# A fused attention-plus-MLP kernel on one core: the first block in two column parts, another load order, a zero tile for warming, and new planner ranks

## Chip, core and metric

The kernel runs on one core of one Trainium2 chip. The metric is the device time of one execution in microseconds; of several executions the median counts. The profile is of one such execution, with its instructions, DMAs and waits.

## What is computed

The input x has 2048 rows (positions) of 640 numbers in bf16. It is normalized row by row, and two branches use the result: an attention over eight earlier positions with a stride of two, and an MLP of width 1536. Their sum with x is the output.

```python
def reference(A_x, A_wqkv, A_wo, B_x, B_w1, B_b1, B_w2, B_b2):
    x = A_x
    xn = _layernorm(x, axis=-1)
    return x + _A_ref(xn, A_wqkv, A_wo) + _B_ref(xn, B_w1, B_b1, B_w2, B_b2)

# A: 32 heads of 20; W, dil = 8, 2
qkv = (x @ wqkv) split into q, k, v per head
logits = einsum("bhsd,bhswd->bhsw", q, kg) * scale     # kg: k at s, s-2, ..., s-14
attn = softmax(where(mask, logits, -1e9))
o = einsum("bhsw,bhswd->bhsd", attn, vg);  A = o @ wo
# B
h = gelu(x @ w1 + b1);  B = h @ w2 + b2
```

B_x is not used: both branches work on the normalized A_x.

## The kernel before

The rows go through in four chunks of 512 (n = 0 to 3), each of four blocks of 128 (bl). Most intermediates are kept transposed, with features on the partitions: xnT is the normalized x of a chunk as five column tiles (KT = 5) of 128 features by 512 positions.

Of each chunk these pieces are done. The planner's names for them are given, because the prediction goes by them.

- st, rs, rc, xn: statistics on VectorE, square root on ScalarE, reciprocal on VectorE, and the normalized block. In chunk 0 this is done block by block, and xn on VectorE; in the other chunks the square root is taken for four blocks at once, and xn is on ScalarE.
- tp and tc: in chunk 0 TensorE transposes a block in five steps (L424), and ScalarE copies the result to xnT. In the other chunks tc is a transposing DMA on the queue of SP.
- gj and gc: the q, k and v projections of chunk 0, by block, in five groups of column tiles (GROUPS): g = 0 is q tiles 0 to 3, g = 1 k tiles 0 to 3, g = 2 the last tiles of q and k, g = 3 and 4 are v. ScalarE copies the sums from PSUM. In the other chunks pj and pc do this for a whole chunk, one column tile at a time (five matmuls of 128x512, L463).
- qk and lg: VectorE multiplies q with a shifted k (L513, eight per chunk), and TensorE sums over each head's features (L539).
- m, mx, ex, ss, ri, at: the softmax on VectorE, with the exponential on ScalarE.
- xs and xd: the weights (attn) are copied out to all features of their head, the tile ax, by two DMAs issued by ScalarE and two issued by SP. There is one ax buffer.
- av, ad, ot: VectorE multiplies ax with a shifted v (L612, eight per chunk), adds in three steps (L621) and makes oT (L627). There is one oT buffer.
- f1 and ge: the first MLP matmul (L634, 12 tiles per chunk) and GELU on ScalarE (L645).
- o: for each block the second MLP matmul in four pieces of three hidden tiles, and a fifth piece that adds oT times wo (L665, L667). oc copies the result from PSUM, od adds it to the output in memory.
- xb: VectorE adds b2 to x (L440), and SP writes the chunk to the output (L447). ld is three loads (w2, wo and b2) that SP issues once the four transposes of chunk 1 have been issued (L335 to L337).

The work around the change is ordered by a planner, `Plan.run`, which runs while the kernel is built. Each piece has an engine, an assumed duration, a rank, needs, and buffers. The planner goes forward in its own time and gives each free engine the piece of the lowest rank that can start. The kernel issues its instructions in that order, and each engine then works through its list strictly in order, on real semaphores. RANK holds offsets that are added to the ranks of some pieces; by its entries the whole list is shifted. `land` are the planner's assumptions of when loads have landed. They set the order only; on the chip an instruction waits for the load itself.

The pool psA has four PSUM accumulators ("acc") that transposes, projections and f1 take in turn. So a projection can wait until ScalarE has copied the one that is four back.

Before the first piece, TensorE runs WARM matmuls on the identity tile (L706), whose results aren't used. The identity is made by GpSimd (POOL) in two steps.

Loads are issued at the start, in this order on the queue of SP: x block 0, wq, x blocks 2 and 3, wk, wv, b1, x of chunks 1 to 3, w1 (L321 to L331). x block 1 is issued by ScalarE (L322).

Of the kernel before, what the change touches and what calls it, by code (L numbers as in the profile page):

```python
# [133 lines left out]
LASTB = S // P - 1  # L134
WARM = 40

# [4 lines left out]
RANK = {  # L141
# [3 lines left out]
}  # L145


def make_plan(fns, offsets=RANK):

    pl = Plan(offsets)  # L150
# [6 lines left out]
    def f(kind, *a):  # L157
        return lambda: fns[kind](*a)
# [6 lines left out]
    for n in range(NCH):  # L165
# [6 lines left out]
        for bl in range(BPC):  # L172
            land = (3.2, 3.2, 6.6, 6.6)[bl] if n == 0 else 11.4 + 1.9 * n
            pl.add(f"st{n}{bl}", VE, 1.17, -40 if n else -99, [], f("st", n, bl), after=land)
            if n == 0:
                pl.add(f"rs{n}{bl}", SE, 0.35, -99, [f"st{n}{bl}"], f("sqrt", n, bl, bl + 1), table="sqrt")
                pl.add(f"rc{n}{bl}", VE, 0.17, -99, [f"rs{n}{bl}"], f("rstd", n, bl, bl + 1))
# [3 lines left out]
        for bl in range(BPC):  # L181
            xn, tp = ("xn", n, bl), ("acc", "tp", n, bl)
            pl.add(f"xn{n}{bl}", SE if n else VE, 0.81 if n else 0.42, early + -4.0 if n else -99, [f"rc{n}" if n else f"rc{n}{bl}"], f("xn", n, bl), [xn])
            if n > 0:
                pl.add(f"tc{n}{bl}", DQ, 4.0 if n > 1 else 2.7, early - 3.0, [f"xn{n}{bl}"], f("td", n, bl), [xn, xnT], 21.5)
                continue
            pl.add(f"tp{n}{bl}", PE, 0.3, early + -3.0 if n else -99, [f"xn{n}{bl}"], f("tp", n, bl), [xn, tp])
            pl.add(f"tc{n}{bl}", SE, 0.65, early + -3.0 if n else -99, [f"tp{n}{bl}"], f("tc", n, bl), [tp, xnT])
        if n == 1:
# [3 lines left out]
        if n == 0:  # L193
            for bl in range(BPC):
                for g, parts in enumerate(GROUPS):
                    ps, last = ("acc", "g", bl, g), max(p[0] for p in parts)
                    tos = sum(p[2] - p[1] for p in parts)
                    land = (5.9, 9.2, 11.5)[last]
                    r = -50 + (last == 2)
                    pl.add(f"gj{bl}{g}", PE, 0.28 * tos, r, [f"tc0{bl}"], f("gj", bl, g), [xnT, ps], land)  # L200
                    pl.add(f"gc{bl}{g}", SE, (0.27, 0.54, 0, 0.54)[tos - 1], -50, [f"gj{bl}{g}"], f("gc", bl, g), [ps] + [(q, k, v)[p[0]] for p in parts])
# [70 lines left out]
def kernel(  # L272
# [65 lines left out]


    ident = consts.tile([P, P], BF16, name="ident")  # L340
    make_identity(nc, ident[:])
# [38 lines left out]
    def do_st(n, bl):  # L380
        b = n * BPC + bl
        stats = lnp.tile([P, 2, nc.vector.BN_STATS_DIM], F32, tag="stats", name="stats")
        nc.vector.bn_stats(stats[:, 0, :], x_sb[:, b, 0 : D // 2])  # L383
        nc.vector.bn_stats(stats[:, 1, :], x_sb[:, b, D // 2 : D])
        nc.vector.bn_aggr(mv[:, b, :], stats[:])

# [13 lines left out]

    def do_xn(n, bl):
        b = n * BPC + bl
        xn = lnp.tile([P, D], BF16, tag="xn", name="xn")
        tiles["xn", n, bl] = xn
        if n:
            nc.scalar.activation(
                xn[:], x_sb[:, b, :], ACT.Identity, bias=nmr[:, b : b + 1], scale=rstd[:, b : b + 1]
            )
            return
        nc.vector.tensor_scalar(  # L410
            out=xn[:],
            in0=x_sb[:, b, :],
            scalar1=mv[:, b, 0:1],
            scalar2=rstd[:, b : b + 1],
            op0=ALU.subtract,
            op1=ALU.mult,
        )

    def do_tp(n, bl):
        xn = tiles["xn", n, bl]  # L420
        tp = psA.tile([P, 2 * CH], BF16, tag="acc", name="tp")
        tiles["tp", n, bl] = tp
        for t in range(KT):
            nc.tensor.transpose(tp[:, t * P : (t + 1) * P], xn[:, t * P : (t + 1) * P], ident[:])  # L424

    def do_tc(n, bl):
        xnT = get(("xnT", n), lambda: xtp.tile([P, KT, CH], BF16, tag="xnT", name="xnT"))
        nc.scalar.copy(
            xnT[:, :, bl * P : (bl + 1) * P],
            tiles["tp", n, bl][:, 0 : KT * P].rearrange("p (t m) -> p t m", t=KT),  # L430
        )
# [38 lines left out]

    def do_gj(bl, g):
        if bl == 0 and g == 3:
            bias1()
        cs = slice(bl * P, (bl + 1) * P)
        ps = psA.tile([P, BPC, P], F32, tag="acc", name="gps")
        tiles["gps", bl, g] = ps
        slots = [(which, to) for which, a, b in GROUPS[g] for to in range(a, b)]
        for i, (which, to) in enumerate(slots):
            for ti in range(KT):
                nc.tensor.matmul(  # L480
                    ps[:, i, :],
                    lhsT=wqkv_p[which][:, ti, to, :],
                    rhs=tiles["xnT", 0][:, ti, cs],
                    start=(ti == 0),
                    stop=(ti == KT - 1),
                )

# [251 lines left out]
```

## Time and profile before

| what | us |
|---|---|
| median of 6 runs (216.47 to 217.9) | 217.06 |
| the profiled execution | 218.04 |
| its span, first to last instruction | 215.9 |
| TensorE busy (PE) | 207.2 |
| VectorE busy (DVE) | 180.7 |
| ScalarE busy (ACT) | 107.4 |
| first projection matmul of chunk 0 starts | 7.63 |
| first f1 matmul starts | 25.18 |
| first product with ax starts | 60.95 |
| first oT starts | 82.27 |
| last matmuls end | 212.82 |

How to read it: times of single steps come from the profiled execution and are in microseconds from the start of the span. A line of a timeline holds start, duration, engine, line of the kernel, operation, tile written and tiles read, shapes, count, and in brackets how long the engine idled before and what ended it. A matmul's drawn end lies behind the moment at which the next one starts, since they are pipelined; so the pace of a row of matmuls is read from their starts. The chain that ended last is followed back from the last instruction; a line has start, duration, and what held the chain. PEclk is the granted clock of TensorE in tenths of full speed.

### The profile page before, as it was taken

The page shows a single profiled execution, that of the slowest core. Times are in us where ns is not written, and L with a number is a line of the kernel's source. Part 1 is how long each engine was busy: PE and PEld are TensorE (multiplying, and loading weights), DVE is VectorE, ACT ScalarE, POOL GpSimd, SP SyncE. Part 2 cuts the span into 40 slices and gives each one's busy share as a digit, 9 for nine tenths or more (in the row PEclk, how much of TensorE's full clock was granted, in tenths as well). Part 3 has the DMA queues.
Part 4 walks back from the last instruction along what each step waited for, and adds up shares of the span by engine and source line. Part 5 has one row for each costly group of instructions (what it writes and reads, how often), then busy time and mean ns, then how long its engine had stood idle before and what let it go on. Part 6 is the DMA issues. An engine that isn't in the chain of part 4 may idle for free.

```text
span 215.9 us, 3941 instructions
## 1 busy us (share of the span) xinstructions
PE 207.2 (96%) x1669; PEld 121.0 (56%) x1692; DVE 180.7 (84%) x170; ACT 107.4 (50%) x190; POOL 14.5 (7%) x33
## 2 busy tenths in 40 slices
PE   7799999999999999999999989999999999999994
PEld 7799845554454444655655545566445455555552
DVE  3829999679989999999999999998999999982001
ACT  3676994895928375553176075213763521351210
POOL 2000000000000000100011000111100011101220
PEclk9999999999999999999999999999999999999999
DMA  6999408826972112508120370222112522205223
GB/s 216 365 365 357 87 20 254 322 98 126 250 62 56 35 30 33 152 0 187 44 30 3 39 183 3 30 33 30 16 18 20 174 30 27 29 8 121 33 30 62
DMA packets 21449, 21.49 MB, mean 100 GB/s; under 512 B 9016, under 2 KB 18616, under 8 KB 21432
## 3 DMA queue, kind: packets, MB, share of 16 engines
q1 hardware_dynamic: 17832, 16.49, 27.7%
q0 software_dynamic: 2160, 2.46, 9.7%
q10 hardware_dynamic: 1440, 2.29, 3.7%
q8 instruction: 13, 0.21, 0.4%
q14 instruction: 4, 0.03, 0.1%
HBM read 10.00 MB, written 5.08 MB: 70 GB/s over the span
## 4 chain that ended last, share of the span: by engine, by line
PE 51%; DVE 29%; DMA 13%; SPq 2%; issue 2%; ACTq 1%; ACT 1%; DVEq 0%
PE lo L665 18%; PE hps L634 14%; DVE pv L612 10%; PE gps L480 8%; DMA ax<-attn 6%; PE hi L667 6%; DMA b2bc<-in_B_b_dram 5%; DVE pv L621 4%; DVE prod L513 3%; PE pps L463 3%; DVE ssum L574 3%; DVE x_sb L440 2%; DVE attn L586 2%; DMA x_sb<-in_A_x_dram 1%; DVE rs L581 1%
## 5 line engine op out<-in xcount | busy, mean ns | idle before, releaser
L634 PE MATMUL hps<-xnT,w_sb 128*128 128x512 bf16 x236 | 54.2, 379 | 0.2
L665 PE MATMUL lo<-w_sb,hT 128*128 128x512 bf16 x183 | 51.9, 379 | 0.0
L612 DVE TENSOR_TENSOR pv<-vT,ax 128x2560 bf16<-128x2560 bf16 x32 | 45.8, 1485 | 1.3 <-DMA ax<-attn 1.3
L513 DVE TENSOR_TENSOR prod<-qT,kT 128x2560 bf16<-128x2560 bf16 x32 | 45.5, 1483 | 0.1
L667 PE MATMUL hi<-w_sb,hT 128*128 128x128 bf16 x192 | 40.3, 219 | 0.5
L645 ACT ACTIVATE hT<-hps,b1T 128x512 bf16<-128x512 f32 x48 | 31.6, 686 | 15.6 <-PE hps L634 13.6
L634 PEld LDWEIGHTS <-w_sb 128*128 128x128 bf16 x240 | 22.9, 98 | 26.5
L621 DVE TENSOR_TENSOR pv<-pv 128x5120 bf16<-128x5120 bf16 x12 | 33.8, 2822 | 0.3
L665 PEld LDWEIGHTS <-hT 128*128 128x128 bf16 x192 | 18.7, 98 | 22.7 <-issue 0.6
L672 ACT CAST osb<-lo 128x512 bf16<-128x512 f32 x15 | 8.8, 585 | 42.7 <-issue 22.8
L678 POOL DMA_DIRECT2D out_dram<-osb x15 | 13.1, 873 | 195.1 <-ACT osb L673 195.1
L665 PE MATMUL lo<-wo,oT 128*128 128x512 bf16 x77 | 22.6, 379 | 0.0
L667 PEld LDWEIGHTS <-hT 128*128 128x128 bf16 x192 | 18.4, 98 | 1.5
L463 PE MATMUL pps<-xnT,wv_sb 128*128 128x512 bf16 x72 | 17.4, 379 | 1.2 <-ACT vT L498 1.0
L463 PE MATMUL pps<-xnT,wq_sb 128*128 128x512 bf16 x75 | 16.8, 379 | 0.6 <-ACT qT L498 0.6
L667 PE MATMUL hi<-wo,oT 128*128 128x128 bf16 x80 | 16.9, 219 | 0.3 <-issue 0.2
L463 PE MATMUL pps<-xnT,wk_sb 128*128 128x512 bf16 x71 | 16.9, 380 | 0.3
L498 ACT CAST vT<-pps 128x512 bf16<-128x512 f32 x15 | 8.2, 595 | 12.4 <-PE pps L463 12.4
L383 DVE BATCH_NORM_STATS2 stats<-x_sb 128x6 f32<-128x320 bf16 x16 | 7.3, 459 | 8.3 <-DMA x_sb<-in_A_x_dram 8.2
L686 DVE TENSOR_TENSOR osb<-lo,x_sb 128x512 bf16<-128x512 f32 x1 | 0.7, 691 | 16.1 <-PE lo L665 16.1
L463 PEld LDWEIGHTS <-wv_sb 128*128 128x128 bf16 x75 | 8.6, 118 | 8.6 <-issue 1.7
L463 PEld LDWEIGHTS <-wq_sb 128*128 128x128 bf16 x75 | 8.8, 117 | 8.2 <-issue 0.9
(63 smaller groups left out, 210.9 us busy)
## 6 DMA issues: line engine op xcount, KB each, us to landing
w_sb<-in_B_w_dram SPq DMA_DIRECT2D x2, 1920.0 KB, 11.8
out_dram<-osb POOLq DMA_DIRECT2D x15, 160.0 KB, 3.4
ax<-attn ACTq DMA_DIRECT2D x8, 256.0 KB, 5.9
ax<-attn SPq DMA_DIRECT2D x8, 256.0 KB, 5.3
x_sb<-in_A_x_dram SPq DMA_DIRECT2D x3, 640.0 KB, 11.6
out_dram<-x_sb SPq DMA_DIRECT2D x3, 640.0 KB, 3.5
wq_sb<-in_A_wqkv_dram SPq DMA_DIRECT2D x1, 800.0 KB, 4.9
wk_sb<-in_A_wqkv_dram SPq DMA_DIRECT2D x1, 800.0 KB, 7.0
```

Source lines behind the costliest of these rows:

```text
L463: nc.tensor.matmul(ps[:], lhsT=wqkv_p[which][:, ti, to, :], rhs=xnT[:, ti, :], start=(ti == 0), stop=(ti == KT - 1),)
L480: nc.tensor.matmul(ps[:, i, :], lhsT=wqkv_p[which][:, ti, to, :], rhs=tiles["xnT", 0][:, ti, cs], start=(ti == 0), stop=(ti == KT - 1),)
L498: nc.scalar.copy(dest[:, to, off : off + CH], tiles["pps", n, which, to][:])
L513: nc.vector.tensor_tensor(out=prod[:, i, :, :], in0=qkv_tile(n, 0)[:], in1=qkv_tile(n, 1)[:, :, off : off + CH], op=ALU.mult,)
L612: nc.vector.tensor_tensor(out=pv[:, i, :, :].rearrange("p t (j c) -> p t j c", j=BPC), in0=qkv_tile(n, 2)[:, :, off : off + CH].rearrange( ...
L621: nc.vector.tensor_tensor(out=ta[:], in0=ta[:], in1=tb[:], op=ALU.add)
L634: nc.tensor.matmul(ps[:], lhsT=w1_sb[:, ti, ft * P : (ft + 1) * P], rhs=tiles["xnT", n][:, ti, :], start=(ti == 0), stop=(ti == KT - 1),)
L645: nc.scalar.activation(hT[:], tiles["hps", n, ft][:], ACT.Gelu_apprx_tanh, bias=b1T[:, ft : ft + 1], scale=1.0)
L665: nc.tensor.matmul(lo[:], lhsT=lhs, rhs=rhs[:, 0:CH], start=first, stop=last)
L667: nc.tensor.matmul(hi[:, 0 : D - CH], lhsT=lhs, rhs=rhs[:, CH:D], start=first, stop=last)
L672: nc.scalar.copy(osb[:, 0:CH], tiles["lo", n, bl][:])
L678: nc.gpsimd.dma_start(rows, tiles["osb", n, bl][:], accum_op=ALU.add)
```

## The change

- x block 0 is loaded in two halves of 320 columns, one issued by SP and one by ScalarE; x block 1 moves to SP, ahead of wq. wk moves ahead of x blocks 2 and 3.
- The statistics piece st becomes two pieces of the planner: one bn_stats, then the other with the aggregation. The instructions are the same.
- For block 0 of chunk 0, xn, the transposes and their copy are done in two parts, of two and of three column tiles. The first group of projections (q tiles 0 to 3 of block 0) is split the same way: the piece ga00 does the first two column tiles for four sums, and gj00 the other three.
- The warming matmuls read a tile of zeros, written by VectorE, and are 43 instead of 40.
- `land` values of the planner change, and RANK is replaced. With this the lists of all engines are in another order in the later chunks too.

```diff
-WARM = 40
+WARM = 43
...
 RANK = {
-    "ad02": 35.3, "av1": -101.7, "av2": 76.7, "f10": 53.1, "f11": 23.2, "f12": 66, "f13": 190, "gj1": -337.3,
-    "gj3": -98.6, "o01": -72.1, "o03": 12.1, "o22": 213.2, "pj11": -45.8, "pj30": 109.2, "pj32": 49.6, "qk1": 10.4,
-    "qk2": 112.3, "rc1": -399, "st2": 79.8, "xb1": -67.6, "xb3": 55.5, "xn1": 47.4,
+    "ad20": 56.1, "av2": 44.3, "f12": 105.7, "f13": 59.6, "gj3": 51.8, "o00": -60.3, "o03": -36.9, "o11": -26,
+    "o22": 162.1, "o33": 269.3, "pad": -4.9, "pc11": 97.1, "pj10": -77.5, "pj11": -121.4, "pj12": -21.6, "pj31": 10.4,
+    "pj32": 7, "qk2": 19.1, "qk3": -38.6, "rc1": -43.7, "st2": 77.6, "st3": 44.1, "xb2": -27.9,
 }
...
-            land = (3.2, 3.2, 6.6, 6.6)[bl] if n == 0 else 11.4 + 1.9 * n
-            pl.add(f"st{n}{bl}", VE, 1.17, -40 if n else -99, [], f("st", n, bl), after=land)
+            land = (3.2, 3.6, 9.0, 9.0)[bl] if n == 0 else 11.4 + 1.9 * n
+            r = -40 if n else -99
+            pl.add(f"st{n}{bl}a", VE, 0.5, r, [], f("st", n, bl, 0), after=land)
+            pl.add(f"st{n}{bl}", VE, 0.62, r, [f"st{n}{bl}a"], f("st", n, bl, 1))
...
-            pl.add(f"tp{n}{bl}", PE, 0.3, early + -3.0 if n else -99, [f"xn{n}{bl}"], f("tp", n, bl), [xn, tp])
-            pl.add(f"tc{n}{bl}", SE, 0.65, early + -3.0 if n else -99, [f"tp{n}{bl}"], f("tc", n, bl), [tp, xnT])
+            for i, (a, b) in enumerate(((0, 2), (2, KT)) if bl == 0 else ((0, KT),)):
+                u = "a" if b < KT else ""
+                us = (b - a) / KT
+                pl.add(f"xn{n}{bl}{u}", VE, 0.06 + 0.36 * us, -99, [f"rc{n}{bl}"], f("xn", n, bl, a, b), [xn])
+                pl.add(f"tp{n}{bl}{u}", PE, (0.54 if bl == 0 else 0.3) * us, -99, [f"xn{n}{bl}{u}"], f("tp", n, bl, a, b), [xn, tp])
+                pl.add(f"tc{n}{bl}{u}", SE, 0.16 + 0.49 * us, -99, [f"tp{n}{bl}{u}"], f("tc", n, bl, a, b), [tp, xnT])
...
-                    land = (5.9, 9.2, 11.5)[last]
+                    land = (5.9, 8.4, 11.5)[last]
                     r = -50 + (last == 2)
-                    pl.add(f"gj{bl}{g}", PE, 0.28 * tos, r, [f"tc0{bl}"], f("gj", bl, g), [xnT, ps], land)
+                    need, cut = [f"tc0{bl}"], 0
+                    if bl == 0 and g == 0:
+                        cut = 2
+                        need.append(pl.add("ga00", PE, 0.112 * tos, r, ["tc00a"], f("gj", bl, g, 0, cut), [xnT, ps], land))
+                    pl.add(f"gj{bl}{g}", PE, 0.056 * (KT - cut) * tos, r, need, f("gj", bl, g, cut, KT), [xnT, ps], land)
...
-    nc.sync.dma_start(x_sb[:, 0, :], x_nb[:, 0, :])
-    nc.scalar.dma_start(x_sb[:, 1, :], x_nb[:, 1, :])
+    nc.sync.dma_start(x_sb[:, 0, 0 : D // 2], x_nb[:, 0, 0 : D // 2])
+    nc.scalar.dma_start(x_sb[:, 0, D // 2 : D], x_nb[:, 0, D // 2 : D])
+    nc.sync.dma_start(x_sb[:, 1, :], x_nb[:, 1, :])
     for s in range(3):
         nc.sync.dma_start(wqkv[s][:], wqkv_v[:, :, s * D : (s + 1) * D])
-        if s == 0:
+        if s == 1:
             nc.sync.dma_start(x_sb[:, 2:BPC, :], x_nb[:, 2:BPC, :])
...
+    zeros = consts.tile([P, P], BF16, name="zeros")
+    nc.vector.memset(zeros[:], 0.0)
...
-            nc.tensor.matmul(idle[:, 0:P], lhsT=ident[:], rhs=ident[:], start=True, stop=True)
+            nc.tensor.matmul(idle[:, 0:P], lhsT=zeros[:], rhs=zeros[:], start=True, stop=True)
```

The functions that do the pieces (do_st, do_xn, do_tp, do_tc, do_gj) take the column range as arguments. In do_gj a split group goes through its column tiles in the outer loop, and marks only the first and the last matmul of the whole group as start and stop.

More of the change, by code (lines that the diff above doesn't have):

```diff
@@ L182, in make_plan @@
             xn, tp = ("xn", n, bl), ("acc", "tp", n, bl)
-            pl.add(f"xn{n}{bl}", SE if n else VE, 0.81 if n else 0.42, early + -4.0 if n else -99, [f"rc{n}" if n else f"rc{n}{bl}"], f("xn", n, bl), [xn])
             if n > 0:
+                pl.add(f"xn{n}{bl}", SE, 0.81, early + -4.0, [f"rc{n}"], f("xn", n, bl), [xn])
                 pl.add(f"tc{n}{bl}", DQ, 4.0 if n > 1 else 2.7, early - 3.0, [f"xn{n}{bl}"], f("td", n, bl), [xn, xnT], 21.5)
                 continue
-            pl.add(f"tp{n}{bl}", PE, 0.3, early + -3.0 if n else -99, [f"xn{n}{bl}"], f("tp", n, bl), [xn, tp])
-            pl.add(f"tc{n}{bl}", SE, 0.65, early + -3.0 if n else -99, [f"tp{n}{bl}"], f("tc", n, bl), [tp, xnT])
+            for i, (a, b) in enumerate(((0, 2), (2, KT)) if bl == 0 else ((0, KT),)):
[4 more added lines that the diff above has]
+                pl.add(f"tc{n}{bl}{u}", SE, 0.16 + 0.49 * us, -99, [f"tp{n}{bl}{u}"], f("tc", n, bl, a, b), [tp, xnT])
         if n == 1:
@@ L377, in get, with do_st @@
         return tiles[key]
-    def do_st(n, bl):
+    def do_st(n, bl, i):
         b = n * BPC + bl
[L382 to L385, printed above, removed]
+        stats = get(("stats", b), lambda: lnp.tile([P, 2, nc.vector.BN_STATS_DIM], F32, tag="stats", name="stats"))
+        nc.vector.bn_stats(stats[:, i, :], x_sb[:, b, i * (D // 2) : (i + 1) * (D // 2)])
+        if i:
+            nc.vector.bn_aggr(mv[:, b, :], stats[:])
     def do_sqrt(n, b0, b1):
@@ L399, in do_rstd, with do_xn @@
             constants()
[L401 to L404, printed above, removed]
+    def do_xn(n, bl, a=0, b=KT):
+        i, cs = n * BPC + bl, slice(a * P, b * P)
+        xn = get(("xn", n, bl), lambda: lnp.tile([P, D], BF16, tag="xn", name="xn"))
         if n:
             nc.scalar.activation(
-                xn[:], x_sb[:, b, :], ACT.Identity, bias=nmr[:, b : b + 1], scale=rstd[:, b : b + 1]
+                xn[:], x_sb[:, i, :], ACT.Identity, bias=nmr[:, i : i + 1], scale=rstd[:, i : i + 1]
             )
@@ L410, in do_xn @@
         nc.vector.tensor_scalar(
[L411 to L414, printed above, removed]
+            out=xn[:, cs],
+            in0=x_sb[:, i, cs],
+            scalar1=mv[:, i, 0:1],
+            scalar2=rstd[:, i : i + 1],
             op0=ALU.subtract,
@@ L417, in do_xn, with do_tp, do_tc @@
         )
-    def do_tp(n, bl):
+    def do_tp(n, bl, a, b):
         xn = tiles["xn", n, bl]
-        tp = psA.tile([P, 2 * CH], BF16, tag="acc", name="tp")
-        tiles["tp", n, bl] = tp
-        for t in range(KT):
+        tp = get(("tp", n, bl), lambda: psA.tile([P, 2 * CH], BF16, tag="acc", name="tp"))
+        for t in range(a, b):
             nc.tensor.transpose(tp[:, t * P : (t + 1) * P], xn[:, t * P : (t + 1) * P], ident[:])
-    def do_tc(n, bl):
+    def do_tc(n, bl, a, b):
         xnT = get(("xnT", n), lambda: xtp.tile([P, KT, CH], BF16, tag="xnT", name="xnT"))
         nc.scalar.copy(
-            xnT[:, :, bl * P : (bl + 1) * P],
-            tiles["tp", n, bl][:, 0 : KT * P].rearrange("p (t m) -> p t m", t=KT),
+            xnT[:, a:b, bl * P : (bl + 1) * P],
+            tiles["tp", n, bl][:, a * P : b * P].rearrange("p (t m) -> p t m", t=b - a),
         )
@@ L469, in do_pj, with do_gj @@
             )
-    def do_gj(bl, g):
+    def do_gj(bl, g, a, b):
         if bl == 0 and g == 3:
@@ L474, in do_gj @@
         cs = slice(bl * P, (bl + 1) * P)
[L475 to L486, printed above, removed]
+        ps = get(("gps", bl, g), lambda: psA.tile([P, BPC, P], F32, tag="acc", name="gps"))
+        slots = [(which, to) for which, lo, hi in GROUPS[g] for to in range(lo, hi)]
+        pairs = [(i, ti) for i in range(len(slots)) for ti in range(a, b)]
+        if b - a < KT:
+            pairs.sort(key=lambda p: p[1])
+        for i, ti in pairs:
+            which, to = slots[i]
+            nc.tensor.matmul(
+                ps[:, i, :],
+                lhsT=wqkv_p[which][:, ti, to, :],
+                rhs=tiles["xnT", 0][:, ti, cs],
+                start=(ti == 0 and (i == 0 or b == KT and a == 0)),
+                stop=(ti == KT - 1 and (i == len(slots) - 1 or b == KT and a == 0)),
+                skip_group_check=True,
+            )
     def do_gc(bl, g):
```

## Prediction

> **What bounds the kernel now.** I read the page's first part, then the chain that ended last in order of time, then the timelines of the engines around its steps.
>
> ```profile
> PE 207.2 (96%) x1669; PEld 121.0 (56%) x1692; DVE 180.7 (84%) x170; ACT 107.4 (50%) x190; POOL 14.5 (7%) x33
> PEclk9999999999999999999999999999999999999999
> ```
>
> TensorE is busy for 96% of the span, so a gain must come from its gaps, and there are few. In its timeline, lines that start later than the one above them ended:
>
> ```profile
> 6.40 1.01 PE L424 MATMUL tp<-ident,xn 128*128 128x128 bf16 x10 [0.76 <-DVE xn L410]
> 7.63 2.39 PE L480 MATMUL gps<-xnT,wq_sb 128*128 128x128 bf16 x40 [0.23 <-ACT xnT L428]
> ...
> 52.30 1.24 PE L463 MATMUL pps<-xnT,wv_sb 128*128 128x512 bf16 x5 [0.31 <-ACT vT L498]
> ...
> 75.99 1.24 PE L463 MATMUL pps<-xnT,wq_sb 128*128 128x512 bf16 x5 [0.62 <-ACT qT L498]
> ...
> 125.49 1.24 PE L463 MATMUL pps<-xnT,wv_sb 128*128 128x512 bf16 x5 [0.70 <-ACT vT L498]
> ```
>
> The bracket hides part of a loss, since a drawn matmul (379 ns) is longer than the pace (five 128x512 matmuls start 1.08 us apart). By the pace the last three cost 0.70, about 0.85 and 0.86 us. But the chain shows that TensorE does not decide alone:
>
> ```profile
> 25.61 4.06 PE hps L634 x18
> ...
> 30.28 0.91 ACT xn L406
> ...
> 33.99 10.69 DMA b2bc<-in_B_b_dram
> 44.71 1.49 DVE x_sb L440
> 46.20 1.87 DVE ssum L574
> ...
> 53.78 7.15 DMA ax<-attn
> ...
> 62.36 4.30 DVE pv L612 x3
> ...
> 78.01 1.49 DVE prod L513
> 79.50 2.75 DVE pv L621
> 82.27 1.49 DVE oT L627
> ```
>
> From 30 to 84 us the end is carried by ScalarE's normalization of chunk 1, the loads queued behind its transposes, VectorE's softmax, the copies that expand the attention weights (ax), and VectorE's products up to oT. oT ends at 83.76, and TensorE's matmuls on oT start at 83.82: there VectorE sets TensorE's time, whatever was lost before. Work moved on this chain counts in full; work off it does not.
>
> **The change, step by step**, against the profiled execution: 218.04 us, span 215.9, so 2.1 us lie around the span. It is 0.98 us above the median of 217.06.
>
> *Start.* x block 0 landed at 3.70 (0.74+2.96), block 1 at 3.88: 0.18 us for 160 KB, so half of block 0 less in front is worth 0 to 0.18; I take 0.1. VectorE's order stays: statistics of blocks 0 and 1, then the reciprocal (5.76), now at 5.66. Split xn: a 128x1 reciprocal takes 0.11, the 128x640 xn 0.44, hence 0.24 and 0.31 for 256 and 384 columns, 0.11 more than one. That delays xn of block 1 by what the landing saved, so its transposes still start at 6.95 and end their issue at 7.25. They stand in TensorE's order before the first projection matmul, whose own input (copy of two column tiles, 0.36 on the line through the casts of 0.27 for 128 and 0.58 for 512 elements) is ready near 6.8. wq landed at 6.07, and no bytes are added before it; one more issue (0.45) is. So projections start at 7.25 instead of 7.63: 0.4 earlier; bounds 0 and 0.6.
>
> *Block 0 to f1.* From 7.63 to 25.18 TensorE was dense (300 projection matmuls, 10 transposes, the bias transpose: 17.55 us). wk landed at 9.25 and x blocks 2 and 3 at 6.99; they swap, so the blocks land by 9.25, 2.26 later, and their xn (9.72) ends near 11.98. TensorE reaches the transpose of block 2 after 90 matmuls of 0.056: 7.25+5.03=12.28. Covered by 0.3 us. So f1 of chunk 0 starts near 24.8 (25.18 before).
>
> *Warming.* Cold matmuls started 107 ns apart from 1.55 to 5.15 and then 56. The zero tile needs one VectorE memset (POOL's of the same tile took 0.20) instead of the two POOL steps that ended at 1.49, so warming starts near 1.0, and 43 matmuls end near 5.0 if 3.6 us warm the clock again. The gap to the first transposes (6.1) is then 1.1 us; the gap before was 0.97 us and the clock held, so the row nearest says that it holds again. Cost: nothing, covered by the wait for x. The other bound, if a zero tile did not warm the clock: 3.6 us of cold running from 6.1 lose 1.8 us. No row speaks for that; the identity tile is nearly all zeros too.
>
> [...]
>
> *What the start is worth at the chain.* xn of block 3 of chunk 1 (30.28) waits in ScalarE's order behind the fourth GELU, which waited for TensorE (29.70) after 0.25 us of idling. The ScalarE work before it starts at the square root at 23.32, which waits for statistics of x that landed from 14.90 on; bytes in front of these are unchanged. After that root the list holds the same sorts of casts, xn, table load and three GELUs as before, so it ends at 29.45. TensorE's 0.4 thus shrinks to 0.25 (bounds 0 and 0.3). The loads of w2, wo and b2, xb0, the sums and attn of chunk 0 follow in the same order: attn ends at 50.06 instead of 50.31, and ax lands at 60.7 instead of 60.93.
>
> *The new orders.* RANK moves most of the later pieces; I go by the order in which the changed planner lists them for each engine. (1) One v projection's copy moves ahead of ScalarE's two ax issues (50.34 to 51.62), so the loss of 0.70 at 52.30 goes. (2) VectorE now does five products L513 before it waits for ax, not six; it idles from 58.4 to 60.7, where it idled 0.83 us. (3) Between ax and oT stand 8 L612 and 3 L621, without the one L513 (1.41) that stood there. So oT starts at 82.27-0.25-1.41=80.6 and ends at 82.1. (4) TensorE's first matmuls on oT now stand after 44 pieces of 1.08 us since f1 began, not 46. From 24.8: 44 x 1.08, three logits of 1.21, two mask matmuls and four output pieces of 0.82 are 54.6 us: TensorE is there at 79.4 and waits until 82.15. The losses at 52.30 and 75.99 vanish into this wait: 2.7 us are late next.
>
> *From there on.* Before, TensorE ran from 83.82 to the last matmul's issue at 212.66, 128.84 us, with one loss of 0.86 (125.49). That one came from ScalarE: its ax issue for chunk 2 (122.50, 2.32 us) waited until VectorE had read the only ax buffer, and held back four copies of v. Now VectorE's last such read ends at 122.39-0.25+1.41+2.83=126.4 (one L513 deferred, one L621 moved ahead), the issue ends at 128.7, the copy at 129.3. In front of that v projection TensorE now has, from 82.15 on, 20 pieces of 1.08, three logits of 1.21 and 18.5 us of output pieces, 43.7 in all; it starts at 125.9 and needs the fifth accumulator at 130.2. So it doesn't wait. Remaining: 128.84-0.86+2 x 1.08=130.14. New small waits: oT of chunk 1 ends near 133.5, and TensorE comes for it at 133.4; the logits of chunk 3 also meet their product within 0.1 us; an accumulator or output buffer is late by 0.07 to 0.2 in a few places. Bounds 0 and 0.8; I take 0.4, between the 0.1 of single waits and their sum.
>
> Sum: 82.15+130.14+0.4=212.7, against 212.66. The span stays at 215.9, the profiled execution at 218.0, and the median at 217.1 us. All that TensorE saves, it waits for at oT.
>
> **The rivals.**
> 1. *TensorE alone decides (faster).* Then 0.4+0.70+0.85+0.86=2.8 us go: 214.3. For it: 96% busy. Against: oT's 83.76 and 83.82.
> 2. *ax lands sooner (faster).* From SP's first ax issue (52.18) to the last landing took 8.75 us; for chunk 1 it was 7.3 (97.26 to 104.58). The wait at oT gives back each us of this one for one, up to 2.7: 217.1-1.45=215.65. Against: the share of DMA time in this window is 0.94, since 640 KB of output go in the same queue, and they still do.
>
> ```profile
> 51.00:61.00 10.00, 9.64 (x81) 4.90 (x81) 9.17 (x8) 7.88 (x13) 0.00 (x0) 1.00 0.94 189
> ```
>
> 3. *VectorE falls behind (slower).* The place is the stretch from ax to oT of chunk 1, where nothing is left: VectorE starts it with 2.3 us of idling behind it, and a product more to do. Each us by which ax lands later, or by which an L612 waits more, goes to the end. It decides from 0.65 us on. If ax takes the 8.75 us plus the 1.5 by which the two ways above differ, 218.5. For it: margins of 0.1 at two later places. Against: neither queue in front of ax has got more work.
> 4. *The order of the loads costs (slower).* If x blocks 2 and 3 landed with wv (11.49) instead of 9.25, the block-2 transposes would come 1.9 us late, and after the covers of 0.25 some 1.6 us would reach the chain: 218.7. It needs a landing after 9.8.
>
> **How the numbers follow.** 0.3% is 0.65 us, about what a measurement can tell from no change. The forecast case, within that, has 0.5. Rival 1 has 0.07, rival 2 0.19, rivals 3 and 4 and a cold clock together 0.24. The range goes from rival 2's end to just short of rival 3's, 215.7 to 218.3; it leaves out rival 1 and about half of the slow cases, 0.19. Faster 0.26, same 0.5, slower 0.24.
>
> **What would show it.** In the changed kernel's profile: first projection matmul near 7.25; f1 near 24.8; warm pace before 6 us; attn of chunk 0 ending near 50.1; VectorE idle over 2 us before the first L612, released by ax; TensorE idle 2 us or more before the first output matmul on oT, near 82.1; no wait at the v projections of chunk 3. I am wrong if TensorE does not wait for oT, if ax lands a microsecond off 60.7, or if the first stage runs cold.

## The result, and the profile after

The changed kernel is slower. Its median is 219.49 us over 28 runs, against 217.19 us over 63 runs of the kernel before. The ratio is **1.0089, interval 1.0073 to 1.0104**, some 1.9 us; it compares only runs within 1.5% of their kernel's fastest, 22 of the 28 here. The forecast was 217.1 us with a range of 215.7 to 218.3, so it was wrong, and on the side to which it gave 0.24. The profiled execution took 219.12 us, its span 217.2.

The page of the changed kernel, first the busy times and then the granted clock in 40 slices of the span:

```profile
PE 206.9 (95%) x1671; PEld 120.8 (56%) x1695; DVE 180.9 (83%) x172; ACT 109.3 (50%) x193; POOL 14.5 (7%) x33
...
PEclk9999999999999999999999999999999999999999
```

TensorE does the same work (206.9 us busy, 207.2 before) in a longer span (217.2, 215.9 before); the 1.3 us that were added are waits. TensorE's timeline shows the first of them:

```profile
0.99 3.87 PE L721 MATMUL idle<-zeros 128*128 128x128 bf16 x43 [0.99 <-DVE zeros L353]
5.55 0.63 PE L436 MATMUL tp<-ident,xn 128*128 128x128 bf16 x5 [0.69 <-DVE xn L423]
6.39 0.45 PE L436 MATMUL tp<-ident,xn 128*128 128x128 bf16 x5 [0.21 <-DVE xn L423]
8.53 2.43 PE L494 MATMUL gps<-xnT,wq_sb 128*128 128x128 bf16 x40 [1.69 <-DMA wq_sb<-in_A_wqkv_dram]
...
14.43 0.45 PE L436 MATMUL tp<-ident,xn 128*128 128x128 bf16 x5 [0.64 <-DVE xn L423]
...
26.96 6.21 PE L649 MATMUL hps<-xnT,w_sb 128*128 128x512 bf16 x27
...
77.26 5.77 PE L475 MATMUL pps<-xnT,wk_sb 128*128 128x512 bf16 x24 [0.58 <-ACT qT L513]
83.69 0.39 PE L680 MATMUL lo<-wo,oT 128*128 128x512 bf16 x1 [0.66 <-DVE oT L642]
```

The transposes come 0.85 earlier than before (5.55 against 6.40), and the projections 0.90 later (8.53 against 7.63): wq was there at 8.49, not at 6.07. The transposes of block 2 wait another 0.64, and the first matmul of f1 starts at 26.96, 1.78 later than before. The chain that ended last carries this on:

```profile
2.70 8.94 DMA x_sb<-in_A_x_dram
11.67 0.90 DVE stats L397 x2
...
14.43 0.45 PE tp L436 x5
...
15.83 11.29 PE gps L494 x200
...
31.48 0.69 ACT hT L660
32.17 0.81 ACT xn L419
...
35.77 10.11 DMA b2bc<-in_B_b_dram
45.91 1.49 DVE x_sb L452
...
53.39 6.92 DMA ax<-attn
...
82.14 1.50 DVE oT L642
83.69 0.39 PE lo L680
```

It now begins with x blocks 2 and 3 (landed at 11.64), goes through f1 and ScalarE's GELU and xn to the load of b2 (45.88), and from there on through the same steps as before, each about 1.2 us late: ax is usable at 62.22 instead of 60.95. Only the new order of VectorE, with one product less in front of oT, brings oT's end back to 83.63, where it was (83.76). From there TensorE needs 130.28 us to its last matmul's end at 213.97; before it was 129.0. That is 1.15 of the 1.3.

In the traces each of these loads has 16 landing marks; what one mark stands for is called a part here. In the profiles of before and after, wq's parts landed so:

| | issued | 8th of 16 | 15th | last |
|---|---|---|---|---|
| before | 1.20 | 5.87 | 6.05 | 6.07 |
| after | 1.66 | 6.41 | 7.40 | 8.49 |

A last part is late again in every load queued behind: wk 10.76 (before 9.25), wv 13.90 (11.49), x of chunk 1 15.71 (14.90). Which of the 16 it is, the marks do not tell.

### The profile page after: what moved, and what is told of

It is laid out like the page before. It is cut to its first block, busy times and chain, and to the rows that moved or that the text cites. A ratio compares the mean times of both kernels' runs of the same rounds, so it can differ in the third digit from the quotient of the medians.

```text
span 217.2 us, 3949 instructions
## 1 busy us (share of the span) xinstructions
PE 206.9 (95%) x1671; PEld 120.8 (56%) x1695; DVE 180.9 (83%) x172; ACT 109.3 (50%) x193; POOL 14.5 (7%) x33
## 3 DMA queue, kind: packets, MB, share of 16 engines
q10 hardware_dynamic: 1440, 2.21, 3.7%
## 4 chain that ended last, share of the span: by engine, by line
PE 67%; DVE 14%; DMA 12%; issue 3%; SPq 2%; ACT 1%; DVEq 0%
PE lo L680 25%; PE hps L649 16%; PE pps L475 10%; PE hi L682 7%; PE gps L494 5%; DMA b2bc<-in_B_b_dram 5%; DVE pv L627 5%; DMA x_sb<-in_A_x_dram 4%; DVE pv L636 4%; DMA ax<-attn 3%; PE L L554 3%; DVE x_sb L452 1%; DVE ssum L589 1%; DVE stats L397 1%; DVE oT L642 1%
## 5 line engine op out<-in xcount | busy, mean ns | idle before, releaser
L680 PE MATMUL lo<-w_sb,hT 128*128 128x512 bf16 x187 | 52.5, 379 | 0.0
L627 DVE TENSOR_TENSOR pv<-vT,ax 128x2560 bf16<-128x2560 bf16 x32 | 45.7, 1485 | 2.5 <-issue 2.3
L660 ACT ACTIVATE hT<-hps,b1T 128x512 bf16<-128x512 f32 x48 | 31.1, 686 | 13.4 <-PE hps L649 10.8
L680 PE MATMUL lo<-wo,oT 128*128 128x512 bf16 x74 | 22.1, 379 | 0.7 <-DVE oT L642 0.7
L397 DVE BATCH_NORM_STATS2 stats<-x_sb 128x6 f32<-128x320 bf16 x32 | 13.6, 464 | 7.4 <-DMA x_sb<-in_A_x_dram 7.4
L475 PE MATMUL pps<-xnT,wv_sb 128*128 128x512 bf16 x72 | 16.7, 379 | 0.2
L680 PEld LDWEIGHTS <-oT 128*128 128x128 bf16 x80 | 7.8, 98 | 10.5 <-DVE oT L642 1.1
L475 PEld LDWEIGHTS <-wk_sb 128*128 128x128 bf16 x75 | 8.7, 118 | 8.1 <-issue 1.2
L419 ACT ACTIVATE xn<-x_sb,nmr,rstd 128x640 bf16<-128x640 bf16 x12 | 11.1, 923 | 3.5 <-DMA xnT<-xn 3.5
```

What stands on the lines that cost most here:

```text
L397: nc.vector.bn_stats(stats[:, i, :], x_sb[:, b, i * (D // 2) : (i + 1) * (D // 2)])
L419: nc.scalar.activation(xn[:], x_sb[:, i, :], ACT.Identity, bias=nmr[:, i : i + 1], scale=rstd[:, i : i + 1])
L475: nc.tensor.matmul(ps[:], lhsT=wqkv_p[which][:, ti, to, :], rhs=xnT[:, ti, :], start=(ti == 0), stop=(ti == KT - 1),)
L627: nc.vector.tensor_tensor(out=pv[:, i, :, :].rearrange("p t (j c) -> p t j c", j=BPC), in0=qkv_tile(n, 2)[:, :, off : off + CH].rearrange( ...
L660: nc.scalar.activation(hT[:], tiles["hps", n, ft][:], ACT.Gelu_apprx_tanh, bias=b1T[:, ft : ft + 1], scale=1.0)
L680: nc.tensor.matmul(lo[:], lhsT=lhs, rhs=rhs[:, 0:CH], start=first, stop=last)
```

## The experiments

In the tables "cold" counts executions whose mean granted clock was 0.989 to 0.992, of those compared: half speed for the 3.41 us that the clock rows of e2, e3, e14 and e15 show (below) is 0.8% of the span. Of the kernel before, beside which the experiments ran, 3 of 104 were so; of the changed kernel 4 of 22, and of all its 28 executions nine had 0.992 or less (one of them 0.983). So the clock is not the loss itself: the 18 of the 22 in which it stayed open have a median of 219.2, beside 217.19 before.

**The four quarters: loads against the rest**

e1 is the changed kernel with the loads of before:

```diff
-    nc.sync.dma_start(x_sb[:, 0, 0 : D // 2], x_nb[:, 0, 0 : D // 2])
-    nc.scalar.dma_start(x_sb[:, 0, D // 2 : D], x_nb[:, 0, D // 2 : D])
-    nc.sync.dma_start(x_sb[:, 1, :], x_nb[:, 1, :])
+    nc.sync.dma_start(x_sb[:, 0, :], x_nb[:, 0, :])
+    nc.scalar.dma_start(x_sb[:, 1, :], x_nb[:, 1, :])
...
-        if s == 1:
+        if s == 0:
```

> The changed kernel with the loads as they were before the change (x block 0 whole on SP, block 1 issued by ScalarE, x blocks 2 and 3 ahead of wk); column parts, zero tile and ranks stay changed. In the changed kernel's profile wq's last of 16 parts landed at 8.49 us where the sum had 6.1, and the first projection matmul stood at 8.53. Theory L (the loads cost it all, the new order breaks even): wq lands near 6.1, projections start near 7.2, f1 near 24.8, ratio to the kernel before 0.997 to 1.003. Theory O (the new order of the pieces costs by itself): the ratio stays at 1.006 or more, with a first stage as in the kernel before.

e2 is the kernel before with this turned round: the loads of the changed kernel and nothing else of it.

> The kernel before with nothing but the changed loads (halves of x block 0, block 1 on SP, wk ahead of x blocks 2 and 3); its own ranks and pieces. Theory L: wq lands after 8 us or x blocks 2 and 3 after 9, and the kernel gets 1 to 2 us slower, ratio 1.005 to 1.01. Its planner also asks for block 2 earlier in TensorE's order than the changed one does, so a wait at the block-2 transposes comes on top. Theory O: within 0.3% of before.

e3 is the changed kernel with only `if s == 1` set back to `if s == 0` (halves and x block 1 on SP stay). e4 is the changed kernel with only the first three lines set back (wk ahead of x blocks 2 and 3 stays).

> The changed kernel with only the swap undone: x blocks 2 and 3 are ahead of wk again, the halves of block 0 and block 1 on SP stay. If the halves (more, smaller rows in front of wq, and wq third on SP's queue) make wq late: wq lands near 8.5, projections start after 8 us, ratio 1.006 or more. If the swap is what costs: wq lands near 6.1 and the ratio is near 1.

> The changed kernel with only the halves undone: block 0 whole on SP, block 1 issued by ScalarE, but wk ahead of x blocks 2 and 3. If the halves are what costs: wq lands near 6.1, x blocks 2 and 3 near 9.3, no wait at the block-2 transposes, ratio 0.997 to 1.003. If the swap costs: the block-2 transposes come late and the ratio is 1.006 or more.

| | ratio, interval | wq's last part | x blocks 2, 3 | first projection | cold |
|---|---|---|---|---|---|
| e1, old loads | 1.0033, 1.0001 to 1.0066 | 5.98 | 7.16 | 7.48 | 4 of 12 |
| e2, new loads alone | 1.0114, 1.0083 to 1.0146 | 8.34 | 11.50 | 8.38 | 1 of 6 |
| e3, halves, x1 on SP | 1.0113, 1.0078 to 1.0148 | 8.82 | 9.72 | 8.87 | 1 of 6 |
| e4, wk ahead | 1.0060, 1.0030 to 1.0090 | 6.85 | 10.04 | 7.42 | 6 of 12 |

The loads alone make the kernel before slower by as much as the whole change does, and without them nearly all of the loss is gone. e1 lies just above theory L's 1.003; its eight executions that are not cold have a median of 217.1, that of the kernel before. Of the two load edits, the first is the dear one. e4 did reach the ratio that was expected if the swap costs, 1.006, but its transposes of block 2 waited only 0.22, and its ratio comes mostly from the clock: the six cold executions have a median of 219.3, the six others 217.6. In e2's profile the late wq costs more than its lateness:

```profile
5.75 1.01 PE L425 MATMUL tp<-ident,xn 128*128 128x128 bf16 x10
8.38 4.05 PE L481 MATMUL gps<-xnT,wq_sb 128*128 128x128 bf16 x40 [1.62 <-DMA wq_sb<-in_A_wqkv_dram]
```

Forty projection matmuls took 4.05 us here and 2.43 in the changed kernel's profile. Matmul starts in e2 are 56 ns apart until 6.54, and 107 ns from 8.56 to 11.86: in the pause TensorE's clock closed.

**The short rows or the place in SP's queue**

e7 is the kernel before with x block 1 on SP, x block 0 whole:

```diff
-    nc.scalar.dma_start(x_sb[:, 1, :], x_nb[:, 1, :])
+    nc.sync.dma_start(x_sb[:, 1, :], x_nb[:, 1, :])
```

> The kernel before, with x block 1 issued by SP ahead of wq instead of by ScalarE; x block 0 stays one load of 1280-byte rows. It tells the place in SP's queue from the short rows. Theory Q (the third place in the queue makes wq late): wq's last part lands near 8.4, first projection near 8.4, ratio near 1.010. Theory R (the 640-byte rows of the halves do it): wq lands within 0.5 of its issue's delay, by 6.6, first projection by 7.9, ratio at most 1.003.

e8 is the kernel before with the halves, and x block 1 as ScalarE's second load, so that wq stays second on SP:

```diff
-    nc.sync.dma_start(x_sb[:, 0, :], x_nb[:, 0, :])
+    nc.sync.dma_start(x_sb[:, 0, 0 : D // 2], x_nb[:, 0, 0 : D // 2])
+    nc.scalar.dma_start(x_sb[:, 0, D // 2 : D], x_nb[:, 0, D // 2 : D])
     nc.scalar.dma_start(x_sb[:, 1, :], x_nb[:, 1, :])
```

> The kernel before, with x block 0 in two halves (SP and ScalarE) and x block 1 issued by ScalarE behind its half; wq stays second on SP. Theory Q: wq lands as before, 6.0 to 6.3, first projection near 7.6, ratio within 0.003 of 1. Theory R: some of wq's 16 parts land 1 to 2.5 us behind the rest, first projection 8.2 or later, ratio near 1.010.

e13 is the kernel before with 128 bytes loaded by SP between x block 0 and wq. e14 is e7 and e15 the changed kernel, each profiled once more.

```diff
     nc.scalar.dma_start(x_sb[:, 1, :], x_nb[:, 1, :])
+    tiny = consts.tile([1, 64], BF16, name="tiny")
+    nc.sync.dma_start(tiny[:], x_nb[0:1, 0, 0:64])
```

> The kernel before, with a load of 128 bytes, which nothing reads, issued by SP between x block 0 and wq: wq is third and issued at 1.66 instead of 1.20, but hardly a byte is added in front of it. Theory I (the later issue alone makes wq late): wq's last part lands at 7.2 or later, as with x block 1 in that place, ratio near 1.005. Theory B (x block 1's rows in front of wq do it): wq lands by 6.6, ratio within 0.002 of 1.

> A second look at the kernel before with x block 1 on SP ahead of wq, whose wq landed at 7.39 in the first look. If the halves' short rows add to the lateness of the changed kernel (8.2 to 8.8 in five profiles), wq lands below 8.0 again; if they do not, as late as there.

> A second look at the changed kernel. If wq's late last part belongs to this order of the loads, it lands between 8.0 and 9.0 again, one to four of its 16 parts over 0.5 behind the median part; if it was chance, within 0.3 of the median part.

| | wq issued | 8th part | last part | ratio, interval |
|---|---|---|---|---|
| second on SP (before, e1, e4, e5, e6, e9, e11, e12) | 1.19 to 1.20 | 5.7 to 5.9 | 5.95 to 6.85 | |
| e8, second, x1 on ScalarE beside it | 1.20 | 6.19 | 6.54 | 1.0071, 1.0030 to 1.0111 |
| e13, third, 128 bytes in front | 1.57 | 6.31 | 7.83 | 1.0079, 1.0042 to 1.0116 |
| e7 and e14, third, x1 in front | 1.66 | 6.31, 6.32 | 7.39, 8.34 | 1.0050, 1.0012 to 1.0088 |
| third with halves (after, e15, e2, e3, e10) | 1.66 | 6.28 to 6.44 | 8.16 to 8.82 | |

e7 lay between its theories. e13 decides between them: of x nothing was moved, no short rows were added, and 128 bytes are hardly a load; wq was issued 0.37 later, and its last part came 1.0 to 1.9 later than in any profile in which it was second.

```profile
1.20 0.32 SPq L324 DMA_DIRECT2D tiny<-in_A_x_dram  x1
1.57 0.42 SPq L326 DMA_DIRECT2D wq_sb<-in_A_wqkv_dram  x1
```

So the short rows are out as the cause: e14 is as late without them. One more issue in front of wq is enough. Whether the moment of the issue or the further entry in the queue does it, e13 does not tell apart. Most parts lose about 0.5, hardly more than the issue lost; but from the 8th part to the last there are 1.1 to 2.4 us in the eight profiles with wq third, against 0.2 to 0.4 in five and 1.0 to 1.1 in three (e4, e5, e12) of those with wq second. What holds these up the runs do not show. The trace does have slow packets: in the changed kernel nine of 1280 bytes, started between 2.78 and 3.81, took 0.47 to 0.69 each (two later ones 0.50 and 0.71), where before none that started after 2.25 took over 0.45. But e13 has only one after 2.25 (0.74, at 3.02), so they can't be all of it.

The late part strikes more than once. In e7 and e13 the first projection hardly moved (7.44 and 7.87, before 7.63), but f1 came 1.07 and 1.50 later (26.25 and 26.68): there TensorE also waited 0.75 and 0.73 for wk, whose last part landed at 10.57 and 10.98 (before 9.25).

e8 missed with both theories: with wq second and in time (6.54), x block 1 landed beside it only at 6.27 (3.88 before), and the loss came by that way. In its profile the granted clock is 0.94 and the span 224.3, so only its loads are read.

**The warming and the clock**

e5 is the kernel before with the zero tile and 43 matmuls. e6 is e1 with the identity and 40 matmuls again, so that column parts and new orders are left alone:

```diff
-WARM = 43
+WARM = 40
...
-            nc.tensor.matmul(idle[:, 0:P], lhsT=zeros[:], rhs=zeros[:], start=True, stop=True)
+            nc.tensor.matmul(idle[:, 0:P], lhsT=ident[:], rhs=ident[:], start=True, stop=True)
```

> The kernel before, with only the warming changed: 43 matmuls on a zero tile written by VectorE instead of 40 on the identity. Theory W (the earlier warming sometimes misses the clock): warming starts near 1.0 and its fast pace comes at a moment that varies from execution to execution; in about a third of the executions the mean granted clock is 0.992 instead of 1.0, which is 0.8% of 216 us, 1.7 us, and these executions take 218.8; the median ratio is 1.002 to 1.006. Rival (the warming is harmless, the cold executions come from the new pieces or orders): no execution at 0.992, ratio 1.000.

> The changed kernel with the loads and the warming of before; what stays is the column parts of block 0 and the new orders. If theory W holds: no execution at a clock of 0.992, and the time is the forecast one: ratio 0.998 to 1.001. Rival (the column parts or the new orders cost by themselves): ratio 1.003 or more, and executions at 0.992 as with the new warming.

e9 is e4 with `WARM = 56`. e10 is the changed kernel with the pause before the projections filled:

```diff
     def do_gj(bl, g, a, b):
...
+        if b < KT:
+            fill = psL.tile([P, W, P], F32, tag="L", name="fill")
+            for _ in range(28):
+                nc.tensor.matmul(fill[:, 0, :], lhsT=zeros[:], rhs=zeros[:], start=True, stop=True)
```

> The variant with wk ahead of x blocks 2 and 3 and the halves undone, with 56 instead of 43 matmuls on the zero tile. With 43, half of its executions had a mean granted clock of 0.992 and took some 2 us more. Theory G (where the clock opens early, the warming ends early and the gap before the transposes closes the clock again): the longer warming fills that gap, at most 1 execution in 12 at 0.992, the median falls from 1.006 to 1.000 to 1.003. Rival (the earlier beginning of the warming is at fault, whatever follows it): a third or more of the executions still at 0.992, ratio 1.005 or more.

> The changed kernel with 28 matmuls on the zero tile between the transposes of block 1 and the first projections, into a tile that is not read (1.6 us at the warm pace, about the wait for wq). Theory L (the late loads cost most, the cold clock only some executions): no execution at 0.992 or below, but the median stays near that of the changed kernel's executions at a clock of 1.0: ratio 1.006 to 1.009. Rival C (the cold clock is the cost): ratio 1.000 to 1.003.

| | ratio, interval | cold |
|---|---|---|
| e5, old orders and loads, zero tile | 1.0019, 0.9987 to 1.0052 | 2 of 12 |
| e6, new orders and parts alone | 1.0020, 0.9989 to 1.0051 | 1 of 12 |
| e9, e4 with longer warming | 1.0048, 1.0019 to 1.0077 | 2 of 10 |
| e10, changed kernel, pause filled | 1.0082, 1.0057 to 1.0106 | 0 of 11 |

e10 answers its question: with the pause filled no execution is cold, and the ratio stays at 1.0082, beside 1.0089. The late loads are the cost, the cold clock only a part of some executions. e6 is the case that the prediction forecast: with the loads and the warming as they were, parts and orders change nothing that can be measured; the interval leaves room for 1.1 us. e5's ratio can't be told from 1, and its 2 of 12 against 3 of 104 are too few to charge the zero tile. e9 settles nothing: it lies between its theories.

The second profile of the changed kernel (e15, an execution of 221.14 us) shows another place where the clock closes. First TensorE's timeline and one line of ScalarE's, then windows of 1 us (length, busy us and counts of PE, PEld, DVE, ACT and POOL, granted clock, DMA share, GB/s):

```profile
70.81 5.56 PE L475 MATMUL pps<-xnT,wq_sb 128*128 128x512 bf16 x25
78.59 7.24 PE L475 MATMUL pps<-xnT,wk_sb 128*128 128x512 bf16 x25 [2.22 <-ACT qT L513]
85.67 0.38 PE L680 MATMUL lo<-wo,oT 128*128 128x512 bf16 x1
...
77.81 0.25 ACT L520 COPY vT<-vT 128x70 bf16<-128x70 bf16 x1 [4.05 <-DVE pv L627]
```

```profile
80.00:81.00 1.00, 1.00 (x4) 0.34 (x3) 0.96 (x2) 0.91 (x2) 0.00 (x0) 0.50 0.42 85
...
83.00:84.00 1.00, 1.00 (x7) 0.52 (x5) 0.97 (x2) 1.00 (x3) 0.00 (x0) 1.00 0.00 0
```

By the pace (25 matmuls 0.2158 apart) TensorE could have started at 76.21 and waited 2.38. What it waited for: ScalarE's copies of q stand in its list behind a small copy of v, and that one waits for VectorE's last product with ax (L627). The clock was then at half speed, 25 matmuls took 7.24 instead of 5.56, and TensorE reached oT 0.71 after it had ended (84.96). In the first profile it was there in time. So here a wait that VectorE's work up to oT would have covered cost 0.71, by the half clock behind it. The same wait was 1.83 in e1, 2.1 in e4 and 1.85 in e9, which had 4 of 12, 6 of 12 and 2 of 10 cold executions, but also 1.7 in e10, which had none. Whether their cold executions go when this wait goes, under the new warming and loads, no run here shows.

The clock rows of the traces also give the moments at which the clock opened and closed. In the profiles of before and after it was open for 211.63 and 215.04 us, to behind the last matmul; that is 62 and 63 times 3.41. In e2 and e14 it closed 3.41 after it had opened, in e15 (from about 4.15 to 79.21) 22 times 3.41 after. Counted in such steps from the opening, TensorE's matmuls can be added up by their pace (0.056 for 128 columns, 0.216 for 512):

| step, us | TensorE's work in it | clock after it |
|---|---|---|
| e2, 5.07 to 8.48 | 29% | half |
| e14, 5.23 to 8.64 | 31% | half |
| e15, 75.79 to 79.21 | 30% | half |
| e13, 4.39 to 7.80 | 38% | full |
| e9, 74.67 to 78.09 | 40% | full |
| changed kernel, 3.75 to 7.16 | 44% | full |
| changed kernel, 7.16 to 10.58 | 59% | full |

The five steps behind which it closed (e3 and e8 have the other two) held 18 to 31% of work. Of those behind which it stayed open, the least here is 38%; in the profiles of before and after no step that ends before TensorE's last matmul holds less than 53% and 44%. The length of the pause does not tell these cases apart: 1.84 between two matmul starts in e2, and the clock closed; 1.91 in the changed kernel, from 6.62 to 8.53, and it stayed open. The work in a step does, in these cases: the 1.91 were split by the border at 7.16.

**The chain through ax and oT**

In e6's profile, VectorE's timeline shows what delays ax: the addition of b2 (L449), which waits for its load, stands ahead of the sums of the softmax, although their input was ready at 43.97. A second one stands behind attn, and SP's ax issue (51.36) is queued behind the output write that waits for it (50.92).

```profile
43.90 1.49 DVE L449 TENSOR_TENSOR x_sb<-x_sb,b2bc 128x2560 bf16<-128x2560 bf16 x1 [2.13 <-DMA b2bc<-in_B_b_dram]
45.31 1.93 DVE L586 TENSOR_REDUCE ssum<-e 128x128 f32<-128x1024 bf16 x1
...
60.12 5.70 DVE L624 TENSOR_TENSOR pv<-vT,ax 128x2560 bf16<-128x2560 bf16 x4 [2.21 <-DMA ax<-attn]
...
80.04 1.49 DVE L639 TENSOR_TENSOR oT<-pv 128x2560 bf16<-128x2560 bf16 x1
```

e11 moves the first of these additions (chunk 0's) in e6 to where VectorE idles before ax; e12 moves the kernel before's first (chunk 1's, "xb1") in the same way.

```diff
-        for t in make_plan(fns).run():
+        plan = make_plan(fns).run()
+        late = next(t for t in plan if t["name"] == "xb0")
+        plan.remove(late)
+        plan.insert([t["name"] for t in plan].index("av000"), late)
+        for t in plan:
             t["fn"]()
```

> The column parts and new orders with the loads and the warming of before, and one piece moved: VectorE's addition of b2 to chunk 0 (1.49) comes behind the products of chunk 1 instead of ahead of the sums of the softmax. If the chain through ax and oT decides, as the prediction says: the sums start when the exponential ends, 43.97 instead of 45.31; attn ends near 48.2, ax lands near 58.8, oT ends near 80.2, and TensorE's wait of about 1.0 at oT and what else hangs on it goes; ratio 0.990 to 0.996. If TensorE alone decides: ratio within 0.002 of 1.

> The kernel before with the same move: the addition that waits for b2 at 44.71 (its first, of chunk 1) comes behind the six products instead of ahead of the sums. If the chain decides: attn ends 1.0 to 2.0 earlier than 50.31, oT ends 1 to 1.7 earlier than 83.76, TensorE's output matmuls follow, ratio 0.992 to 0.996. If TensorE alone decides: ratio within 0.002 of 1.

The ratios to the kernel before are 0.9955 (0.9931 to 0.9978) for e11 and 0.9958 (0.9933 to 0.9982) for e12: medians 216.38 and 216.41 beside 217.34. Neither had a cold execution in 12. VectorE in e11:

```profile
43.87 1.94 DVE L586 TENSOR_REDUCE ssum<-e 128x128 f32<-128x1024 bf16 x1 [2.23 <-ACT e L581]
...
56.56 1.48 DVE L449 TENSOR_TENSOR x_sb<-x_sb,b2bc 128x2560 bf16<-128x2560 bf16 x1
58.87 5.70 DVE L624 TENSOR_TENSOR pv<-vT,ax 128x2560 bf16<-128x2560 bf16 x4 [0.83 <-DMA ax<-attn]
...
78.78 1.49 DVE L639 TENSOR_TENSOR oT<-pv 128x2560 bf16<-128x2560 bf16 x1
```

The sums start 1.44 earlier, the first product with ax 1.25, oT 1.26. TensorE's matmuls on oT start at 80.33 instead of 81.59, and its last five at 210.18 instead of 211.43: 1.26 and 1.25. The chain gives back its time one for one. e11 is faster than both kernels. In e12 oT starts 0.68 earlier than before (81.59 against 82.27), and its matmuls (83.14) follow TensorE's previous ones without a wait: there the two meet. They had met before too, as these lines of TensorE's timeline before the change show, for five matmuls 0.216 apart from 82.68 also end at 83.76, with oT:

```profile
82.68 1.24 PE L463 MATMUL pps<-xnT,wv_sb 128*128 128x512 bf16 x5
83.82 0.39 PE L665 MATMUL lo<-wo,oT 128*128 128x512 bf16 x1
```

TensorE could come earlier in e12 because its wait for the copies of q (0.8 before) was gone. The gain at oT stayed under the 1 to 1.7 that were expected: the moved addition, started at 58.88, now stands right in front of the first product with ax (60.28).

## Why the prediction was wrong

**Start: the step that failed.** It said of wq: "no bytes are added before it; one more issue (0.45) is", and took 6.07 for the landing, so that the projections would start at 7.25. The transposes did end in time (6.84 drawn, forecast 7.25 for the issue), and here the prediction was too low: for block 0's earlier landing it took 0.1, at most 0.18, and the halves landed at 2.94 and 3.13 instead of 3.70. e7 shows 3.01 with block 0 whole, so it was the move of x block 1, not the halving, that brought this. But wq landed at 8.49: the one more issue was counted at nothing, since 6.07+0.45 still lay before 7.25, and it meant a landing at 7.39 to 8.82 in the eight profiles that have it, against 5.95 to 6.85 in nine that don't (e8 among them). The term was mis-sized because a landing was read as issue plus a constant, when the projections waited for the last of 16 parts (8.49; the 8th had landed at 6.41).

**Block 0 to f1.** "so the blocks land by 9.25" was the second mis-sized term: 11.64, 2.4 late, by a late last part again (the 8th landed at 9.55). With wq in time (e4) they landed at 10.04, and the transposes then waited 0.22, not the 1.9 of a landing with wv; so the swap has a price of its own, a small one. f1 started at 26.96 instead of 24.8; 1.28 of this is the late start of the projections, about 0.8 the wait at the transposes of block 2 (13.57 to 14.43 between matmul starts).

**What the start is worth at the chain.** "bytes in front of these are unchanged" held, and x of chunk 1 still landed 0.81 later, at 15.71. Attn's end came 1.46 after the forecast one (51.52 against 50.06), ax's first product 1.5 after (62.22 against 60.7).

**The new orders: right.** From ax to oT's end the changed kernel took 21.4 us, as forecast (60.7 to 82.1); from oT to the end 130.28, where 130.14 and 0.4 were forecast; the wait at the v projections of chunk 3 was gone; VectorE idled 2.29 before ax. Of the 2.7 us that TensorE was to wait at oT, e1 shows 1.83 ahead of the k projections and 1.04 at oT, 2.87 together. So "the losses at 52.30 and 75.99 vanish into this wait" was half right: the second one grew, and in e15 it cost 0.7 through the clock.

**Warming.** "Cost: nothing" can't be refuted (e5). The warm pace did come before 6 us in both profiles of the changed kernel (3.74 and 4.15), but in e1, e5 and e10 all 43 warming matmuls ran cold, and in e1 the pace turned only near 7.1. The prediction looked for the danger in the beginning of the warming; the clock closed later, in the pauses that the loads (at 8.48 in e2) and the new orders (at 79.21 in e15) made.

**The rivals.** Rival 4 is what happened, by its place (the order of the loads) and its condition (x blocks 2 and 3 after 9.8). Its price (218.7, measured 219.49) came near by luck: it had 1.9 at the transposes of block 2, where 0.8 were lost, and nothing at wq. Its reason was another too, since wk in front of these blocks accounts only for the 9.25 that was forecast. Rival 3 did not happen in the first profile: VectorE's stretch took what was forecast. In e15 its condition did: the first product with ax came 11.91 after attn's end, 10.70 in the first profile, and oT ended 1.33 later. In e1, e4 and e9 it took 11.6 too, in most others 10.5 to 10.8; why is open. Rival 1's premise is refuted by e11 and e12: the kernel gets faster when VectorE's chain does, and no TensorE work is touched. But the two times that the prediction set against it, 83.76 and 83.82, did not show it, since TensorE's own work ended there too. Rival 2's mechanism is confirmed by e11: the 1.25 by which the first product with ax came earlier came back as 1.25 at the last matmuls.

The sum, then, in the first profile: forecast 82.1 for oT, 1.5 late by the loads, is 83.6; and 130.3 from there is 213.97 against the forecast 212.7, 1.3 us. The executions beyond the profiled one lose more, by a later ax (63.56 in e15) and by cold stretches; the median is 2.4 above the forecast.

## What to carry to other kernels

Here the first projection waited for the slowest part of its load (wq 8.49, start 8.53; the 15th part was there at 7.40): before moving an issue in front of another, look at all the landing marks of both, and give the one pushed back, and those queued behind it, a bound from the spread of the parts, not from the issue's length. When a pause of TensorE looks free because something else ends later, ask what the clock does after it: in e15 25 matmuls took 7.24 us instead of 5.56 behind one of 2.38. And where a profile says 96% busy, the chain through the slower engines may still be where a cheap piece can be moved for a gain: here one addition that waited for a load stood in front of work that was ready, and its move gave a ratio of 0.9955 (e11).

## What was not expected of the hardware

- With one more issue in front, 0.37 to 0.46 us, the last of 16 parts of an 800 KB load came 0.5 to 2.9 us later (7.39 to 8.82 in eight profiles, 5.95 to 6.85 in nine), and a last part was late in the loads behind it on the queue too (wk 10.76 in the changed kernel, 9.25 before). e13 shows that neither short rows nor more than 128 bytes in front are needed for it. Why is open.
- TensorE's clock closed in the 1.84 us between two matmul starts in e2, in the 2.21 in e3 and in the 2.38 of the wait in e15; in the changed kernel's first profile it stayed open over 1.91. In these cases the step of 3.41 us ahead of the closing, counted from the opening, held 18 to 31% of work; steps with 38% (e13), 40% (e9) and 44% (the changed kernel) left it open. Shares in between were not measured, and why the work in a step should count, no run here shows. Once closed, it stayed so for one step (3.41 by the clock rows of e2, e3, e14 and e15).
